# Moving the first dense layer of a gated convolution and MLP kernel into its FFT stage, handover and first period

## The chip, the cores and the metric

The kernel runs on one core of one Trainium2 chip. A core has five engines, each with an instruction queue of its own that runs in order: TensorE (matrix products, written to PSUM), VectorE and ScalarE (elementwise work), GpSimd (called POOL in the profile; here it fills buffers and issues DMA transfers) and SyncE (SP; it only issues transfers). Transfers between the chip's memory (DRAM) and the on-chip buffer are issued on the queues of SP, ScalarE and POOL. The metric is the time of one execution on the device, in microseconds; lower is better.

## The reference

A gated mix of a long convolution `a` (a diagonal state-space model, done by FFT) and a two-layer MLP `b`, and the gradients of all its inputs. L = 2048 positions, D = 448 channels, N = 256 states, F = 1792 hidden units; data in bf16.

```python
def _B_ref(x, w1, b1, w2, b2):
    h = jnp.einsum("bsd,df->bsf", x, w1) + b1
    zero = jnp.zeros_like(h)
    r = jnp.where(h > zero, h, zero)
    h = r * r
    out = jnp.einsum("bsf,fd->bsd", h, w2) + b2
    return out

x = A_u
g = _sigmoid((x * gate_w).sum(-1, keepdims=True))
a = _A_ref(x, A_A_re, A_A_im, A_B_re, A_B_im, A_C_re, A_C_im, A_log_dt, A_Dskip)
b = _B_ref(x, B_w1, B_b1, B_w2, B_b2)
return g * a + (1 - g) * b
...
_out, _vjp = jax.vjp(_f, A_u, A_A_re, A_A_im, A_B_re, A_B_im, A_C_re, A_C_im, A_log_dt, A_Dskip, B_w1, B_b1, B_w2, B_b2, gate_w)
_grads = _vjp(grad_out)
```

`_A_ref` builds the kernel K of each channel from powers of `exp(dt * A)` and convolves u with it. What matters below: `r` (the relu of the first layer, needed again in the backward pass) and `r * r`, which feeds the second product.

## The kernel before

The program has five stages. Times are those of the profiled execution.

- **Start** (to about 88 us): inputs, the gate, the first FFT step of u and of the incoming gradient (`fwd1`), and `UT`, which is u transposed, in a buffer `SB`.
- **FFT stage** (88 to 181 us; lines 560 to 626). `powers(gr)` squares a table of complex numbers twelve times, for four groups of chunks; ScalarE and VectorE take turns, and a record of each chunk goes to `rec_d`. `spectra(q)` loads a quarter of both signals from `gd`, does the second FFT step on TensorE (`fwd2`, line 265) and copies the results out of PSUM (lines 218, 219, 228, 230). `products` multiplies the two spectra on VectorE (line 288), and `inv1` does the first step back on TensorE (line 303) and stores to `hd`. In this stage the order in each queue comes from a planner, which places instructions by estimated durations. PSUM banks `X` and `S` are free here.
- **Handover** (181 to 229.6 us). From line 994 on the order is the program's own. `hd` and the record of chunk 1 are loaded on SP's queue (lines 998 and 1015), then all of w1 into `w1w` (lines 1020 to 1022). Tables for chunks 0 and 1 are built, sums of `hd` are formed on TensorE (line 1037), turned through DRAM and loaded back as `DK`.
- **Periods 1 to 13** (229.6 to 568.7 us). The 448 channels form 14 chunks. Period c builds tables of chunk c on VectorE (`X0` to `X2`, `Y0` to `Y4`: lines 656, 657, 670, 673, 679) while chunk c - 1 goes backward: `Z` is a product on TensorE and a ScalarE copy (`back_z`, lines 815 and 817), `T` turns a table (line 773), `P` multiplies on VectorE (lines 827 and 828), `S` sums on TensorE (line 844). ScalarE spreads fields and seeds for the next chunk (lines 688, 689, 709 to 724). The string `PERIOD` (line 1086) is that order written out; `KO` ends the period with a copy (`k_out`, line 760), queues the DMA transposes of the `Y` table on SP (line 779) and calls `release()`, which issues the transfers collected in `behind`. For chunks in `ON_PE` (7 to 12) one of four transposes is done on TensorE, with two ScalarE copies (line 790).
- **Tail** (to the end): weight gradients and the last FFT steps. It reads r back from `rT_d`.

At each of the ten `D` tokens of a period `D_` runs pending steps of the generator `dense()`. The first layer (`first_layer`, lines 896 to 932) runs, for each of four blocks of 512 positions (`lb`), seven steps (`jp`), each for 256 hidden units: eight matrix products (lines 905 and 908) into two PSUM banks, two relus with the bias on ScalarE (line 912), a store of r to `rT_d` on POOL's queue, and, two steps later, its square on VectorE (line 915) into `hblk`. Then `project` multiplies that block by w2 in eight half-steps (line 883), each pair ending with a ScalarE copy (line 887). During the last block's projection `turn_w1` transposes w1 (lines 940 and 941), then `turn_w2` w2. The second layer (`second_layer`) is the backward pass: 28 steps of products (lines 963 and 966), two ScalarE copies (line 968), one VectorE product with r (line 971), and the same projections with w1. In all 127 steps: eight in period 1, and the other 119 by their number, evenly over periods 2 to 13.

## Time and profile before

| | us |
|---|---|
| median of 3 runs (lowest, highest) | 812.92 (811.3, 815.8) |
| the profiled execution | 813.03 |
| its span, first to last instruction | 811.2 |

A profile line names the source line, the engine, the operation and the tiles (`out<-in`, with their types and shapes). "Idle before" is how long the engine stood just ahead of such an instruction, and the name behind the arrow is what it was waiting for. PEclk is the share of TensorE's full clock that the throttle granted: at 0.5 a matrix product takes about twice as long. PEld is TensorE's weight load, which runs beside PE. A name such as `SPq` is a queue's own time for issuing a transfer. Engines overlap, so busy times don't add up to the span; an idle engine costs only where something waits for it.

### The profile page before, as it was taken

The page shows a single profiled execution, that of the slowest core. Times are in us where ns is not written, and L with a number is a line of the kernel's source. Part 1 is how long each engine was busy: PE and PEld are TensorE (multiplying, and loading weights), DVE is VectorE, ACT ScalarE, POOL GpSimd, SP SyncE. Part 2 cuts the span into 40 slices and gives each one's busy share as a digit, 9 for nine tenths or more (in the row PEclk, how much of TensorE's full clock was granted, in tenths as well). Part 3 has the DMA queues.
Part 4 walks back from the last instruction along what each step waited for, and adds up shares of the span by engine and source line. Part 5 has one row for each costly group of instructions (what it writes and reads, how often), then busy time and mean ns, then how long its engine had stood idle before and what let it go on. Part 6 is the DMA issues. An engine that isn't in the chain of part 4 may idle for free. (4 is left out here: it accounts for less than half of the span.)

```text
span 811.2 us, 17087 instructions
## 1 busy us (share of the span) xinstructions
PE 621.9 (77%) x6845; PEld 303.0 (37%) x6845; DVE 612.7 (76%) x947; ACT 539.4 (66%) x879; POOL 162.0 (20%) x264
## 2 busy tenths in 40 slices
PE   3776367663378889988989889989778689898985
PEld 1222122121243334434554444534535234444442
DVE  3795597877834999989789989989657864888263
ACT  0696467670578687968899879884575487465463
POOL 1222000042111132213231001101135311123122
PEclk9986555565688989999989999999989899999998
DMA  9978766279759387968986979895689998999972
GB/s 192 240 204 282 298 244 233 90 286 212 211 109 186 76 198 142 200 124 217 196 158 112 290 175 228 176 246 139 207 274 311 368 294 289 285 301 330 255 218 63
DMA packets 167214, 175.73 MB, mean 217 GB/s; under 512 B 104068, under 2 KB 144990, under 8 KB 166542
## 3 DMA queue, kind: packets, MB, share of 16 engines
q1 hardware_dynamic: 140152, 97.89, 49.9%
q0 software_dynamic: 17552, 56.44, 22.8%
q10 hardware_dynamic: 9430, 20.31, 7.2%
q8 instruction: 53, 0.87, 0.5%
q14 instruction: 27, 0.22, 0.1%
HBM read 83.67 MB, written 67.53 MB: 186 GB/s over the span
## 5 line engine op out<-in xcount | busy, mean ns | idle before, releaser
L817 ACT CAST P<-psF 128x1024 bf16<-128x1024 f32 x56 | 57.2, 1021 | 27.8 <-PE psF L815 27.7
L656 DVE TENSOR_TENSOR F<-X,F 128x1024 bf16<-128x1024 bf16 (+2 forms) x42 | 64.4, 1533 | 9.8 <-ACT X L689 7.3
L883 PEld LDWEIGHTS <-U 128*128 128x128 bf16 x448 | 40.9, 100 | 48.0 <-issue 16.6
L883 PE MATMUL psN<-D,U 128*128 128x448 bf16 x224 | 54.1, 386 | 1.1 <-DMA D<-in_B_w_dram 0.7
L888 POOL DMA_DIRECT2D br_d<-D x32 | 17.5, 548 | 180.0 <-ACT D L887 173.7
L1201 PEld LDWEIGHTS <-S 128*128 128x128 bf16 x416 | 39.0, 99 | 38.6 <-issue 9.3
L1201 PE MATMUL psX<-D,S 128*128 128x449 bf16 x224 | 47.2, 353 | 1.7 <-ACT S L1207 1.5
L883 PE MATMUL psN<-S,U 128*128 128x448 bf16 x224 | 46.8, 353 | 1.5 <-issue 1.3
L963 PE MATMUL psN<-S,K 128*128 128x512 bf16 x168 | 42.4, 386 | 6.0 <-ACT R L790 5.6
L815 PE MATMUL psF<-R,S 41*32 41x256 bf16 x896 | 24.7, 291 | 28.0 <-DVE P L828 17.4
L827 DVE TENSOR_TENSOR M<-P,psF 128x2048 bf16<-128x2048 bf16 x28 | 34.1, 1216 | 14.0 <-PE psF L773 12.5
L905 PE MATMUL psN<-S,K 128*128 128x512 bf16 x168 | 43.1, 395 | 0.0
L1201 PE MATMUL psX<-K,S 128*128 128x448 bf16 x192 | 41.2, 359 | 1.7 <-ACT S L1204 1.7
L1192 ACT ACTIVATE S<-psN 128x1024 bf16<-128x1024 bf16 x32 | 33.0, 1030 | 13.7 <-PE psN L1188 13.6
L303 PE MATMUL psN<-D,cb_MI 64*128 64x448 bf16 x96 | 31.7, 532 | 9.1 <-DVE D L288 5.5
L303 PEld LDWEIGHTS <-cb_MI 64*128 64x128 bf16 x256 | 17.6, 110 | 53.2 <-issue 46.5
L265 PEld LDWEIGHTS <-M 128*64 128x64 bf16 x192 | 13.9, 133 | 62.6 <-issue 54.9
L657 DVE TENSOR_TENSOR X<-F 128x512 bf16<-128x512 bf16 (+2 forms) x42 | 35.6, 847 | 1.4
L968 ACT ACTIVATE U<-psN 128x512 bf16<-128x512 f32 x56 | 31.1, 616 | 7.6 <-PE psN L966 5.3
L796 ACT COPY S<-K 128x128 bf16<-128x128 bf16 x56 | 34.9, 1007 | 0.0
L828 DVE TENSOR_TENSOR P<-P,psF 128x2048 bf16<-128x2048 bf16 x28 | 34.2, 1221 | 1.0
L773 PE MATMUL psF<-ident,X 128*128 128x128 bf16 x448 | 31.8, 228 | 3.0 <-ACT P L817 2.9
(350 smaller groups left out, 1617.3 us busy)
## 6 DMA issues: line engine op xcount, KB each, us to landing
sp<-K ACTq DMA_DIRECT2D x8, 896.0 KB
dhT_d<-U SPq DMA_DIRECT2D x28, 256.0 KB
R<-sp SPq DMA_DIRECT2D x8, 896.0 KB
S<-dhT_d POOLq DMA_DIRECT2D x14, 512.0 KB, 7.3
R<-hd SPq DMA_DIRECT2D x16, 448.0 KB
S<-rT_d POOLq DMA_DIRECT2D x12, 512.0 KB, 7.0
hd<-st SPq DMA_DIRECT2D x13, 448.0 KB
rec<-rec_d POOLq DMA_DIRECT2D x11, 448.0 KB, 4.8
```

The costliest lines, as they stand in the source:

```text
L303: nc.tensor.matmul(ps[kk2][:, 0:D], lhsT=MI[r0:r0 + 64, m, :], rhs=rh[r0:r0 + 64], start=(k_ == 0), stop=(k_ == len(terms) - 1), tile_posi ...
L656: V.tensor_tensor(out=Vt[:, 0:2 * w * n], in0=run(lo, 0, [0, 2], [NA, w], [1, n]), in1=run(PX[:, 0:1], 512 * k, [2, w], [0, n], [1, 2]), o ...
L657: V.tensor_tensor(out=run(lo, n, [NA * X2, 2], [NA, X2], [1, n]), in0=run(vb, 0, [n * X2, 2], [n, X2], [1, n]), in1=run(vb, (w + X2) * n, ...
L796: S.copy(D2[:, :, 0, 4 * l:4 * l + 4].rearrange("p (g i) a -> p a g i", g=NG), DK[:, l::4].rearrange("p a (e g q i) -> p a e q g i", g=NG, ...
L817: S.copy(zbs[c, g // 2][:, :, g % 2].rearrange("p t h k n -> p t k h n"), psz[:].rearrange("p t (k h n) -> p t k h n", k=2, h=2))
L827: V.tensor_tensor(out=pr.rearrange("p t g h k n -> p t (g h k n)"), in0=zv, in1=xv, op=ALU.mult)
L828: V.tensor_tensor(out=zv, in0=zv, in1=rev_dim(xv, 1), op=ALU.mult)
L883: T_.matmul(ps[:, 0:D], lhsT=hblk[:, j, P * tt:P * tt + P], rhs=ws[:, j, :], start=(w == 1 and j == 0), stop=(j == FT - 1))
L905: T_.matmul(pss[k][:], lhsT=w1w[:, dt, j * P:j * P + P], rhs=UT[:, dt, 512 * lb:512 * lb + 512], start=(dt == 0), stop=False, skip_group_c ...
L963: T_.matmul(pss[k][:], lhsT=w2Tw[:, jp, dt, k], rhs=dblk[:, dt], start=(dt == 0), stop=False, skip_group_check=True)
L1192: S.activation(hn(i)[:, 8 * th:8 * th + 8, :], ps[:], ACT.Square if i < FT else ACT.Copy)
L1201: T_.matmul(ps[:, 0:w], lhsT=hn(i)[:, t, :], rhs=(DB2[:, t, :] if i < FT else U[:, t, 0:w]), start=(t == 0), stop=(t == LT - 1))
```

## The change

The 28 steps of the first layer that make r no longer run in the periods. They are now `h_step`, in the order `jp` first, then `lb`: 16 in the FFT stage (between the parts of each quarter), 4 in the handover and 8 in period 1. An `h_step` in the FFT stage does one of its two relus on ScalarE and one on VectorE; the others do both on ScalarE. Each of the seven blocks of w1 has its own buffer and its own loads of 256 columns. r goes to `rT_d`: the first eight stores of the FFT stage on POOL's queue and its other eight on SP's, those of the handover and period 1 on POOL's.

From period 2 on r is loaded back from `rT_d` on SP's queue into six buffers (and one more for the seventh tile), and ScalarE squares it into one of two blocks, during the projection of the block before. The loads that a square's buffer makes possible are collected and issued twice in a period, at `KO` and at the new token `RL`. The whole w1 load moves from the handover to the end of period 1, into the same memory. `turn_w1` runs in the first block's projection instead of the last one's. The loads `load_db` and `load_r` go on SP's queue instead of POOL's. `ON_PE` starts at chunk 2 instead of 7. The remaining steps are spread over periods 2 to 13 by weights (0.3 for the first three steps of squares, 1.0 for a half projection, 0.5 for `turn_w2`, 1.3 for a step of the second layer) instead of by number.

```diff
+    HP = FT // 2
+    W1B = ct["Ew_tile"]
+    w1bs = [RA[:, 7168:8192], SB[:, 11264:12288], Pct_[:, 7168:8192]] + [W1B[:, 4096 + 1024 * i:5120 + 1024 * i] for i in range(4)]
...
+    def load_w1b(jp, q_):
+        wb, f0 = w1bs[jp], 256 * jp
+        q_.dma_start(wb[:, 0:3], bass.AP(tensor=B_w1.tensor, offset=B_w1.offset + f0, ap=[[F, P], [P * F, 3], [1, 256]]))
+        for h in range(2):
+            q_.dma_start(wb[64 * h:64 * h + 64, 3], bass.AP(tensor=B_w1.tensor, offset=B_w1.offset + 384 * F + f0, ap=[[F, 64], [1, 256]]))
+    hleft = [(jp, lb) for jp in range(HP) for lb in range(4)]
...
+    hbanks = [lambda: K.ps("X", [P, 512]), lambda: K.ps("S", [P, 512])]
...
+    def h_step(bks, on_act, q_=None):
+
+        jp, lb = hleft.pop(0)
+        wb = w1bs[jp]
+        pss = [b() for b in bks]
+        for k in range(2):
+            for dt in range(DT - 1):
+                T_.matmul(pss[k][:], lhsT=wb[:, dt, k * P:k * P + P], rhs=UT[:, dt, 512 * lb:512 * lb + 512], start=(dt == 0), stop=False, skip_group_check=True)
+        for k in range(2):
+            h = slice(64 * k, 64 * k + 64)
+            T_.matmul(pss[k][:], lhsT=wb[h, 3, k * P:k * P + P], rhs=UT[h, 3, 512 * lb:512 * lb + 512], start=False, stop=True, tile_position=(64 * k, 0), skip_group_check=True)
+        r = hbuf[hn_[0] % len(hbuf)]
+        hn_[0] += 1
+        for k in range(2):
+            b1 = b1_f[:, 2 * jp + k:2 * jp + k + 1]
+            if on_act[k]:
+                S.activation(r[:, 512 * k:512 * k + 512], pss[k][:], ACT.Relu, bias=b1)
+            else:
+                V.tensor_scalar(out=r[:, 512 * k:512 * k + 512], in0=pss[k][:], scalar1=b1, scalar2=0.0, op0=ALU.add, op1=ALU.max)
+        (q_ or G_).dma_start(pair_rows(rT_d, jp, lb), r.rearrange("p (k l) -> p k l", k=2))
+
+    def H(n=1):
+        for _ in range(n):
+            h_step(hbanks, (True, False), nc.sync if len(hleft) <= 20 else G_)
+    for jp in (3, 4):
+        load_w1b(jp, nc.sync)
     powers(0)
     spectra(0)
     powers(1)
     for q in range(4):
         if q < 3:
             spectra(q + 1)
+        if q == 0:
+            for jp in range(3):
+                load_w1b(jp, G_)
+        H((2, 3, 3, 1)[q])
         for h in range(2):
             K.products(Pct[:, h], spw[:, 2 * (q % 2) + 1, 2 * h:2 * h + 2], spw[:, 2 * (q % 2), 2 * h:2 * h + 2])
             K.inv1(None, q, hd[0], (h,), Pct[:, h])
+            H(1 if (q, h) != (3, 1) else 0)
...
+    def load_rx(i, q):
+        if i < 4 * HP:
+            asked.append(i)
+            q.dma_start(rx_of(i).rearrange("p (k l) -> p k l", k=2), pair_rows(rT_d, i % HP, i // HP))
+
+    def square(i):
+        jp, lb = i % HP, i // HP
+        if i not in asked:
+            release()
+        assert i in asked
+        hb = hblkB if lb % 2 else hvs[0][:, 0:7168].rearrange("p (j l) -> p j l", j=FT)
+        S.activation(hb[:, 2 * jp:2 * jp + 2].rearrange("p k l -> p (k l)"), rx_of(i), ACT.Square)
+        if i != HP - 1:
+            behind.append(lambda: load_rx(i + (7 if i < HP else 6), nc.sync))
...
+        while hleft:
+            h_step([bank, bank], (True, True))
+            yield
...
+        for i in range(HP):
+            behind.append(lambda i=i: load_rx(i, nc.sync))
+        behind.append(lambda: nc.sync.dma_start(w1w[:, 0:3], bass.AP(tensor=B_w1.tensor, offset=B_w1.offset, ap=[[F, P], [P * F, 3], [1, F]])))
...
+        def ex0(k):
+            for v in (2 * k, 2 * k + 1):
+                if v < HP:
+                    turn_w1(v)
+                elif 8 <= v < 8 + HP:
+                    square(HP + v - 8)
...
+        yield from project(0, 0, w2n, ex0)
+        for lb in (1, 2):
+            yield from project(lb, 0, w2n, lambda k, lb=lb: square(HP * lb + HP + k) if k < HP else None)
+        yield from project(3, 0, w2n, ex3)
...
+    first_steps = len(hleft) - 4 + 1
+    cost = [0.3] * 3 + [1.0] * 32 + [0.5] * HP + ([1.3] * HP + [1.0] * 8) * 4
...
+    for jp in (5, 6):
+        load_w1b(jp, nc.sync)
+    del hbuf[:]
+    hbuf += [SB[:, 8192:9216], SB[:, 9216:10240], SB[:, 10752:11776]]
+    for _ in range(4):
+        h_step(hbanks, (True, True))
...
-    PERIOD = """X0 D Z0 Y0 X1 D X2 Z1 D Y1 T0 SA D P0 LR Y2 D Z2 D Y3 Z3 FX0 Y4 FX1 D S0 FY0 T1 D FY1 FY2 XS YS KM P1 YP SV D D KO S1""".split()
+    PERIOD = """X0 D Z0 Y0 X1 D X2 Z1 D Y1 T0 SA D P0 RL LR Y2 D Z2 D Y3 Z3 FX0 Y4 FX1 D S0 FY0 T1 D FY1 FY2 XS YS KM P1 YP SV D D KO S1""".split()
     nd = PERIOD.count("D")
-    ON_PE = range(7, NCH - 1)
+    ON_PE = range(2, NCH - 1)
```

More of the change, by code (lines that the diff above doesn't have):

```diff
@@ L930, in first_layer @@
             if k > 0:
-                load_r(k + 1)
+                load_r(k + 1, nc.sync)
             yield
@@ L953, in second_layer @@
     def second_layer():
-        load_r(7)
+        hblk = hvs[0][:, 0:7168].rearrange("p (j l) -> p j l", j=FT)
+        load_r(7, nc.sync)
         for lb in range(4):
@@ L984 @@
     steps = dense()
-    done, total = 0, 4 * 2 * (HP + 8) + HP
+    first_steps = len(hleft) - 4 + 1
+    cost = [0.3] * 3 + [1.0] * 32 + [0.5] * HP + ([1.3] * HP + [1.0] * 8) * 4
+    cost = [sum(cost[:i + 1]) for i in range(len(cost))]
+    done, total = 0, first_steps + len(cost)
     def D_(want):
@@ L1019 @@
     tables_y(0)
-    nc.sync.dma_start(w1w[:, 0:3], bass.AP(tensor=B_w1.tensor, offset=B_w1.offset, ap=[[F, P], [P * F, 3], [1, F]]))
-    for h in range(2):
-        nc.sync.dma_start(w1w[64 * h:64 * h + 64, 3], bass.AP(tensor=B_w1.tensor, offset=B_w1.offset + 384 * F, ap=[[F, 64], [1, F]]))
     seeds_x(1)
@@ L1070 @@
     dbl = [SB[:, 6272 + 2048 * i:8320 + 2048 * i] for i in range(2)]
-    rr = [hv[:, 7168:8192], st4] + [w2v[:, 1024 * i:1024 * i + 1024] for i in range(6)]
     xst = [0]
@@ L1149 @@
                 k += 1
-                D_(first_steps * k // nd if c == 1 else first_steps + (total - first_steps) * ((c - 2) * nd + k) // (nd * (NCH - 2)))
+                D_(first_steps * k // nd if c == 1 else first_steps + sum(x <= cost[-1] * ((c - 2) * nd + k) / (nd * (NCH - 2)) + 1e-6 for x in cost))
             elif c == 1 and o == "LR":
```

87 lines of the change are left out of this document (48 added, 39 removed).

## The prediction

> **What bounds the kernel now.** The page's first two parts come first: no engine is full over the span, and TensorE's granted clock is down between slices 4 and 12.
>
> ```profile
> PE 621.9 (77%) x6845; PEld 303.0 (37%) x6845; DVE 612.7 (76%) x947; ACT 539.4 (66%) x879; POOL 162.0 (20%) x264
> ...
> PEclk9986555565688989999989999999989899999998
> ```
>
> So the stages have different bounds. I cut the span at the FFT stage (88 to 181 us), the handover (181 to 229.6) and the ends of the 13 periods, which are the `k_out` copies of line 760 on ScalarE. In this view of windows the columns are the stretch, its length, the busy time of each engine with its count, granted clock, DMA share and GB/s.
>
> ```profile
> core 0: us, PE busy (x) PEld busy (x) DVE busy (x) ACT busy (x) POOL busy (x), PEclk, DMA share, GB/s
> 88.00:181.00 93.00, 60.21 (x240) 20.60 (x239) 75.44 (x152) 62.19 (x125) 9.23 (x8) 0.57 0.57 215
> 185.10:205.50 20.40, 8.98 (x85) 3.38 (x89) 12.94 (x15) 0.00 (x0) 2.78 (x2) 0.50 0.95 220
> 229.60:257.90 28.30, 22.08 (x312) 9.56 (x313) 8.80 (x11) 21.70 (x34) 5.42 (x7) 0.87 0.92 180
> 257.90:285.70 27.80, 24.23 (x342) 11.26 (x341) 25.50 (x30) 17.41 (x28) 4.16 (x7) 0.88 0.44 86
> 285.70:311.00 25.30, 22.60 (x309) 9.95 (x308) 24.78 (x30) 20.59 (x33) 7.06 (x11) 0.87 0.93 181
> 311.00:338.40 27.40, 25.39 (x365) 11.93 (x363) 24.83 (x29) 21.91 (x35) 6.49 (x10) 1.00 0.80 174
> 392.60:418.80 26.20, 23.38 (x405) 14.35 (x403) 22.94 (x25) 24.47 (x33) 8.03 (x13) 0.87 0.78 170
> 338.40:546.00 207.60, 183.33 (x2817) 95.12 (x2816) 191.72 (x219) 173.96 (x261) 37.73 (x64) 0.96 0.87 192
> 546.00:568.70 22.70, 21.09 (x328) 10.68 (x328) 20.64 (x23) 11.26 (x20) 3.25 (x6) 0.96 0.58 147
> 257.90:568.70 310.80, 276.64 (x4154) 138.93 (x4153) 287.46 (x328) 245.13 (x371) 58.68 (x97) 0.95 0.81 177
> ```
>
> In periods 2 to 13 (last row) VectorE is busy 287.5 of 310.8 us, 92%: it sets the pace, with TensorE (89%) close behind and ScalarE (79%) with room, but in the period that ends at 418.8 ScalarE is at 24.47 of 26.2, 93%. Period 1 has almost no VectorE work. The second row lies in the handover; two rows of SP's queue and one of ScalarE, in order of time, say what it waits for:
>
> ```profile
> 190.19 0.58 SPq L701 DMA_DIRECT2D M<-rec_d  x1
> ...
> 192.05 0.41 SPq L1020 DMA_DIRECT2D K<-in_B_w_dram  x1
> ...
> 205.53 0.83 ACT L709 COPY F<-M 128x768 bf16<-128x768 bf16 x1 [21.36 <-DMA M<-rec_d]
> ```
>
> Between 185 and 205.5 us ScalarE does nothing, until the record of chunk 1 (`rec_d`) lands behind the `hd` loads in the same queue, and the DMA engines are at 0.95: this stretch is bound by bytes, at 220 GB/s.
>
> **The change part by part.** The prices of one step are read from the groups (count, then busy time in all, mean ns of one):
>
> ```profile
> L720 ACT ACTIVATE F<-rec 128x768 bf16<-128x768 bf16 x26 | 20.7, 852 | 0.0
> L717 ACT COPY F<-rec 128x1536 bf16<-128x1536 bf16 x13 | 19.2, 1479 | 1.8 <-DVE F L673 1.8
> L912 ACT ACTIVATE S<-psN,b_f 128x512 bf16<-128x512 f32 x28 | 18.2, 712 | 3.2 <-PE psN L908 3.1
> L790 ACT COPY R<-psN 128x1024 bf16<-128x1024 bf16 x16 | 17.6, 1164 | 1.1 <-PE psN L789 1.1
> L887 ACT CAST D<-psN 128x448 bf16<-128x448 f32 x32 | 17.5, 546 | 23.1 <-PE psN L883 22.9
> ...
> L941 ACT COPY S<-psN 128x896 bf16<-128x896 bf16 x7 | 6.4, 910 | 4.5 <-PE psN L940 4.4
> ```
>
> ```profile
> L219 DVE CAST K<-psN 128x448 bf16<-128x448 f32 x22 | 13.4, 622 | 19.0 <-PE psN L265 18.8
> L971 DVE TENSOR_TENSOR U<-U,D 128x1024 bf16<-128x1024 bf16 x20 | 13.0, 684 | 1.9 <-ACT U L968 1.9
> ```
>
> One first-layer step costs 0.65 us per ScalarE relu (18.2 / 28), twice, and its square on VectorE 0.65 us (line 971 has the same form). Its TensorE price is read from two steps of period 1, one at half clock, one at full:
>
> ```profile
> 231.15 2.69 PE L905 MATMUL psN<-S,K 128*128 128x512 bf16 x6
> ...
> 234.44 1.47 PE L905 MATMUL psN<-S,K 128*128 128x512 bf16 x6
> 235.84 0.39 PE L908 MATMUL psN<-S,K 64*128 64x512 bf16 x2
> ```
>
> So 1.9 us at full clock and about 3.1 at half.
>
> *FFT stage: +5 us.* Sixteen steps come in, each with one relu on ScalarE (16 x 0.65 = 10.4 us) and one add-and-max on VectorE. The trace has no such instruction; line 219 (448 columns from PSUM, 0.62 us) scaled to 512 columns is estimated at 0.69, so 11 us. VectorE goes from 75.4 to 86.4 of 93 us, ScalarE from 62.2 to 72.6. The longest waits of VectorE there (from 89.7 us; the sum, how often, the longest):
>
> ```profile
> DVE K L219 <- PE psN L265: 11.5, 5, 9.1
> DVE R L593 <- ACT P L591: 2.7, 4, 1.0
> DVE R L593 <- ACT S L591: 2.7, 5, 1.0
> DVE D L288 <- PE psN L303: 2.5, 3, 1.4
> ```
>
> 9.1 us of it is one wait at the start for the `gd` load, the rest is pieces of 1.4 us or less. If all 11 us fill idle time the stage grows by nothing, if none do by 11; I take the middle, 5. TensorE sets a bound above: 16 x 3.1 us at the present 0.57 clock is 50 us on 60.2, 110 for 93, or +17. Against that, the period that ends at 338.4 has TensorE busy 25.39 of 27.4 us with a clock of 1.00, and at full clock the sum is 60 + 30 at most, which fits. The stores and the block loads use a DMA share of 0.57 and queues that idle.
>
> *Handover: +4.8 us.* Four steps run on TensorE and ScalarE, which idle there, so their arithmetic is free. Their four stores are not (the row of DMA issues has their size and the us to landing):
>
> ```profile
> rT_d<-S POOLq DMA_DIRECT2D x14, 256.0 KB, 5.2
> ```
>
> They leave through POOL's queue while the `hd` loads and the record saturate the DMA engines: 1.05 MB / 220 GB/s = 4.8 us. If they land outside the stretch it is 0. The whole w1 load that goes from here stood behind the record in SP's queue, so its removal gives nothing. The DMA page of the Trainium skill ("DMA: Bandwidth & Descriptors", section "Issuing engines are not separate DMA queues") says that transfers from the scalar, sync and gpsimd engines all run on the same 16 engines and interleave. By it a second queue for r adds no bandwidth, and the 0.95 share above agrees.
>
> *Period 1: 0.* Eight steps instead of seven (+1.3 us of ScalarE, which is busy 21.7 of 28.3) against half a projection less; both bounds are under 2 us.
>
> *Periods 2 to 4: +8.5 us.* Twenty-one steps go from periods 2 to 7, but all 28 squares go to ScalarE, and the new weights (0.3, 1.0, 0.5, 1.3; 104.8 in all, 8.73 a period) put 13, 8 and 7 of them in periods 2, 3 and 4, with all seven `turn_w1` in period 2. A square of 1024 columns from SBUF lies between line 720 (768 columns, 20.7 / 26 = 0.80) and line 717 (1536, 1.48): 1.0 us. `ON_PE` from 2 adds two copies of line 790, 2.2 us a period. ScalarE's own work in a period: the three rows have 59.9 us, less 14 steps' relus (28 x 0.65 = 18.2) and some 7.5 projections (x 0.55 = 4.1), over three: 12.5. Then:
> - period 2: 12.5 + 2.2 + 13 + 7 x 0.91 + 3 x 0.55 = 35.7
> - period 3: 12.5 + 2.2 + 8 + 5 x 0.55 = 25.5
> - period 4: 12.5 + 2.2 + 7 + 4 x 0.55 = 23.9
>
> That is 85.1 us of ScalarE for what took 80.5. With no gap it costs 4.6; at the 93% of the fullest period 91.5, or +11. I take 8.5, between them. A late reload holds ScalarE too: what stands behind a square on its queue is `back_z`'s copy, `back_p` on VectorE waits for that, and TensorE's next `back_z` for `back_p`. The r tiles that squares 7 to 12 free are asked for at `KO`, behind that period's transposes on SP, and square 13 is the first step of period 3:
>
> ```profile
> 278.53 16.31 SPq L779 DMA_TRANSPOSE R<-Y  x4
> ...
> 410.28 11.17 SPq L779 DMA_TRANSPOSE R<-R  x3
> ```
>
> With three transposes of 11.2 us from 7 to 9 us before a period's end, the load goes out 2 to 4 us into the next one. I put up to 5 us of this into the range.
>
> *Periods 5 to 13: -6.5 us.* VectorE's own work is (287.5 - 49 x 0.65) / 12 = 21.3 us a period. Periods 5 to 12 now hold 27 products of the second layer: 8 x 21.3 + 27 x 0.65 = 188 against 191.7 us. At the present share (191.7 / 207.6 = 92%) that is -4; with less TensorE and ScalarE work in periods 6 and 7 I take -6, up to -16.5 if VectorE runs with 1.5% gaps. Period 13 loses one product: -0.5.
>
> Sum: 5 + 4.8 + 0 + 8.5 - 6.5 = +11.8. The profiled run took 813.03 us, 1.8 more than its span of 811.2 and level with the median of the runs shown, 812.92. Forecast: **825 us**.
>
> **The rivals.**
> - *Faster, by TensorE: 805 us.* If the other engines wait for TensorE in both stages, its relief pays twice. In the FFT stage full matmuls open the clock and the waits of lines 219 and 288 on it (11.5 - 9.1 and 2.5 us) go, and with them the like on ScalarE: 0 instead of +5. In periods 5 to 12 VectorE runs nearly gapless, -16.5, and period 13 -1; periods 2 to 4 cost only ScalarE's bare content, +4.6, the handover its 4.8: -8. For it: TensorE at 89% of the periods. Against it: VectorE is at 92% already, and most of what it does stays. It decides if period 5, which has no square, falls under 22.5 us. The Trainium skill's page "TensorE: Matmul & The Clock Gate", section "What's actually happening", has the throttle released by activity; the FFT stage's 0.57 beside 0.9 to 1.0 in fuller periods agrees.
> - *No change: 815 us.* The FFT steps find their place (the 9.1 us wait among it) and the stores miss the saturated stretch, so that only the periods' +2 is left. Against it: planned places go by estimates, and the store follows its relu at once.
> - *TensorE binds the FFT stage at half clock: 837 us.* +17 instead of +5. For it: the clock is at half in most of that stage though TensorE is busy 65%, and the work comes in pieces between waits for two banks.
>
> **How the numbers follow.** Forecast 0.40, faster 0.27, no change 0.17, half clock 0.16. The range goes from 4 us under the faster case to the last one with the late reload, 801 to 842; it takes in the bounds of the FFT steps (0 to +17), of the stores (0 to 4.8), of periods 2 to 4 (+4.6 to +16) and of periods 5 to 12 (-16.5 to -4), though not all at one end. Faster or slower counts from 0.5%, 4 us, which is about what a measurement of this kernel can tell. Faster 0.27, same 0.17, slower 0.56 (forecast and half clock).
>
> **What would show it.** Right: the FFT stage 3 to 8 us longer with VectorE above 85 us; the record landing 4 to 5 us later after the last `hd` store; period 2 above 34 us with ScalarE over 90%, and periods 5 to 12 near 25. Wrong: period 2 under 31 us, where squares would cost less or lie in gaps; an FFT stage that doesn't grow; periods 5 to 12 under 24 us, where TensorE was the pace.

## The result: slower by 3.9%, and where the 36 us lie

The changed kernel takes 844.05 us (median of four runs, 837.0 to 849.34), the kernel before 812.11 beside it: ratio 1.0386, interval 1.0294 to 1.0478. The direction was forecast, the size wasn't: 825 was predicted, and 844 lies just outside the range that ended at 842.

The profiled execution took 849.34 us, with a span of 847.6 (811.2 before). Both spans are cut at the same places of the program: the FFT stage ends with the issue of its last `hd` store, and a period ends with its `k_out` copy (line 760 before, 811 after); period 1 begins at the end of the first of these copies.

| stretch | before | after | difference | forecast |
|---|---|---|---|---|
| FFT stage, to the last `hd` store | 180.8 | 203.7 | +22.9 | +5 |
| handover, to period 1 | 49.6 | 51.3 | +1.7 | +4.8 |
| period 1 | 27.9 | 28.3 | +0.4 | 0 |
| periods 2 to 4 | 80.6 | 91.6 | +11.0 | +8.5 |
| periods 5 to 13 | 230.2 | 227.6 | -2.6 | -6.5 |
| tail | 242.1 | 245.1 | +3.0 | 0 |

The tail is not touched by the change and scatters: in the eighteen runs below it took 235 to 245 us.

Of the page of the changed kernel, the busy times and the granted clock by slices:

```profile
PE 643.2 (76%) x6896; PEld 313.3 (37%) x6925; DVE 606.6 (72%) x935; ACT 566.6 (67%) x901; POOL 154.3 (18%) x254
...
PEclk9975678579858697999799989999979799999999
```

VectorE went from 76% of the span to 72% and the time still grew: some work was taken from it (612.7 to 606.6 us), and it waits longer. The view of windows, with the columns as in the prediction (the FFT stage from 89.7 us, then periods 1, 2, 3, 5 and 6, then periods 2 to 13 together):

```profile
89.70:204.00 114.30, 92.57 (x361) 28.13 (x364) 85.64 (x168) 71.10 (x138) 18.93 (x19) 0.74 0.58 211
...
254.90:283.30 28.40, 23.66 (x332) 10.04 (x337) 6.43 (x7) 22.38 (x35) 6.26 (x9) 0.82 0.84 188
283.30:324.20 40.90, 31.21 (x396) 17.05 (x396) 25.55 (x30) 34.43 (x44) 2.88 (x5) 0.79 0.89 228
324.20:351.30 27.10, 22.87 (x338) 12.49 (x339) 21.15 (x23) 24.92 (x36) 4.35 (x9) 0.87 0.63 150
...
374.80:403.50 28.70, 22.76 (x367) 12.97 (x368) 24.76 (x26) 21.23 (x31) 5.39 (x10) 0.88 0.59 152
403.50:432.90 29.40, 21.59 (x353) 11.51 (x356) 20.95 (x26) 22.85 (x35) 0.00 (x0) 0.83 0.73 137
...
283.30:602.50 319.20, 254.62 (x4037) 136.22 (x4054) 273.10 (x304) 255.28 (x365) 35.95 (x66) 0.90 0.76 179
```

**FFT stage.** VectorE gained 10.2 us (75.4 to 85.6) and ScalarE 8.9 (62.2 to 71.1), nearly what was counted. But the stage is 23 us longer, so VectorE's idle time, which was to take in part of the 10 us, grew as well: from 15.9 us (of 91.3, counted from 89.7) to 28.7.

**Period 2** takes 41 us with ScalarE busy 34.4 of them (forecast: 35.7). The content was right; the idle time around it wasn't. ScalarE's timeline at its start (start, us busy, line, in brackets how long it stood and for what):

```profile
282.79 0.48 ACT L811 CAST P<-psX 128x328 bf16<-128x328 f32 x1
285.59 3.90 ACT L973 ACTIVATE U<-S 128x1024 bf16<-128x1024 bf16 x4 [2.32 <-DMA S<-rT_d]
289.39 0.99 ACT L868 CAST P<-psF 128x1024 bf16<-128x1024 f32 x1
290.28 1.06 ACT L973 ACTIVATE U<-U 128x1024 bf16<-128x1024 bf16 x1
291.24 1.04 ACT L973 ACTIVATE U<-st 128x1024 bf16<-128x1024 bf16 x1
292.19 1.00 ACT L868 CAST P<-psF 128x1024 bf16<-128x1024 f32 x1
293.08 1.06 ACT L973 ACTIVATE U<-S 128x1024 bf16<-128x1024 bf16 x1
296.21 0.91 ACT L1030 COPY S<-psN 128x896 bf16<-128x896 bf16 x1 [2.07 <-PE psN L1029]
297.36 0.91 ACT L1030 COPY S<-psN 128x896 bf16<-128x896 bf16 x1 [0.24 <-PE psN L1029]
```

Four squares (line 973) stand ahead of the first `back_z` copy (line 868), and the first of them waits 2.3 us for its tile of r. So the copy ends at 290.4, and TensorE's next product into bank `F` waits 7.6 us for it (the longest of the eleven waits in the first row of the changed kernel's waits below).

**Periods 2 to 13** together are 8.4 us longer. Three waits there that grew (the sum, how often, the longest), first of the kernel before, then of the changed one:

```profile
PE psF L815 <- ACT P L817: 2.2, 5, 1.0
...
DVE F L656 <- ACT X L689: 7.3, 6, 2.3
...
DVE M L827 <- PE psF L773: 2.9, 3, 1.4
```

```profile
PE psF L866 <- ACT P L868: 20.8, 11, 7.6
...
DVE M L878 <- PE psF L824: 25.5, 8, 7.5
DVE F L707 <- ACT X L740: 11.5, 7, 4.8
```

These are the same three waits under new line numbers. VectorE's busy time fell by 14.4 us (287.5 to 273.1) and its idle time rose by over 22 (23.3 to 46.1): `back_p` waits for a turned table on TensorE (2.9 to 25.5 us), and TensorE waits for ScalarE to empty the bank `F` (2.2 to 20.8).

### The profile page after: what moved, and what is told of

It is laid out like the page before. It is cut to its first block, busy times and chain, and to the rows that moved or that the text cites. A ratio compares the mean times of both kernels' runs of the same rounds, so it can differ in the third digit from the quotient of the medians.

```text
span 847.6 us, 17291 instructions
## 1 busy us (share of the span) xinstructions
PE 643.2 (76%) x6896; PEld 313.3 (37%) x6925; DVE 606.6 (72%) x935; ACT 566.6 (67%) x901; POOL 154.3 (18%) x254
## 5 line engine op out<-in xcount | busy, mean ns | idle before, releaser
L868 ACT CAST P<-psF 128x1024 bf16<-128x1024 f32 x56 | 57.4, 1025 | 28.3 <-PE psF L866 26.0
L866 PE MATMUL psF<-R,S 41*32 41x256 bf16 x896 | 25.7, 302 | 48.8 <-ACT P L868 21.6
L938 PE MATMUL psN<-S,U 128*128 128x448 bf16 x224 | 50.1, 367 | 0.7 <-issue 0.3
L1053 PE MATMUL psN<-S,K 128*128 128x512 bf16 x151 | 42.8, 401 | 5.8 <-ACT R L841 3.7
L938 PEld LDWEIGHTS <-U 128*128 128x128 bf16 x336 | 30.9, 102 | 33.7 <-issue 11.3
L824 PE MATMUL psF<-ident,X 128*128 128x128 bf16 x448 | 33.8, 236 | 8.6 <-ACT P L868 8.5
L901 POOL DMA_DIRECT2D s_d<-st x21 | 11.2, 537 | 137.8 <-ACT st L899 137.8
L824 PEld LDWEIGHTS <-X 128*128 128x128 bf16 x448 | 29.8, 106 | 15.6 <-issue 15.2
L866 PEld LDWEIGHTS <-S 41*32 41x32 bf16 x896 | 9.2, 90 | 65.7 <-issue 37.5
L841 ACT COPY R<-psN 128x1024 bf16<-128x1024 bf16 x26 | 28.9, 1161 | 3.3 <-issue 2.6
## 6 DMA issues: line engine op xcount, KB each, us to landing
dhT_d<-U SPq DMA_DIRECT2D x28, 256.0 KB
D<-rT_d SPq DMA_DIRECT2D x21, 256.0 KB
```

The lines of the kernel that those rows point to most:

```text
L824: T_.transpose(ps[:, t, 128 * b:128 * b + 128], Xs[c % 2][:, o_:o_ + 128], ident[:])
L866: T_.matmul(psz[32 * ii:32 * ii + 32, t, 256 * k:256 * k + 256], lhsT=DKc[64 * t:64 * t + NY, c % 2, CW * g + i].rearrange("p s a -> p (s ...
L868: S.copy(zbs[c, g // 2][:, :, g % 2].rearrange("p t h k n -> p t k h n"), psz[:].rearrange("p t (k h n) -> p t k h n", k=2, h=2))
L938: T_.matmul(ps[:, 0:D], lhsT=hb[:, j, P * tt:P * tt + P], rhs=ws[:, j, :], start=(w == 1 and j == 0), stop=(j == FT - 1))
L1053: T_.matmul(pss[k][:], lhsT=w2Tw[:, jp, dt, k], rhs=dblk[:, dt], start=(dt == 0), stop=False, skip_group_check=True)
```

## The experiments

Each run is an edit of the changed kernel, but the one that says otherwise. The kernel before took 809.9 to 813.5 us (medians) beside them. "Last `hd` store" is the end of its issue; some of the expectations name its start (180.4 and 203.3 for the two kernels). Where an edit leaves out stores of r (e1, e2, e4, e5, e14), rows of r that nobody writes are read from written rows of the same size; this part of the edits is not printed.

| run | last hd store | period 1 begins | periods 1 to 13 | time | ratio (interval) |
|---|---|---|---|---|---|
| before | 180.8 | 230.3 | 338.8 | 812.1 | |
| after | 203.7 | 254.9 | 347.6 | 844.1 | 1.039 (1.029 to 1.048) |
| e1 no steps in the FFT stage | 186.6 | 237.3 | 347.6 | 828.9 | 1.021 (1.015 to 1.028) |
| e2 products only | 187.0 | 237.9 | 350.6 | 832.2 | 1.025 (1.017 to 1.034) |
| e3 relus only | 206.1 | 256.3 | 347.6 | 841.1 | 1.036 (1.028 to 1.044) |
| e4 no stores | 206.0 | 256.0 | 346.9 | 846.6 | 1.043 (1.038 to 1.049) |
| e5 no steps, no loads | 181.8 | 248.5 | 346.0 | 838.4 | 1.033 (1.018 to 1.049) |
| e6 relus on ScalarE | 206.1 | 254.3 | 347.0 | 846.6 | 1.044 (1.033 to 1.054) |
| e7 steps last | 189.5 | 270.8 | 346.7 | 863.7 | 1.065 (1.053 to 1.076) |
| e8 weights | 203.5 | 254.7 | 348.6 | 843.2 | 1.039 (1.028 to 1.051) |
| e9 squares on VectorE | 204.2 | 255.9 | 347.6 | 851.6 | 1.050 (1.040 to 1.060) |
| e10 ON_PE from 7 | 207.9 | 256.7 | 353.6 | 845.0 | 1.042 (1.031 to 1.053) |
| e11 eight in the handover | 206.5 | 264.4 | 350.3 | 855.9 | 1.055 (1.043 to 1.068) |
| e12 squares on GpSimd | 202.7 | 252.2 | 382.6 | 877.1 | 1.082 (1.070 to 1.093) |
| e13 one powers group | 173.3 | 221.3 | 349.1 | 815.7, one run | |
| e14 the same, no steps | 153.9 | 204.0 | 352.0 | 796.0, one run | |
| e15 r loads on POOL | 204.1 | 255.3 | 363.7 | 864.3 | 1.065 (1.060 to 1.070) |
| e16 before, half the squares on ScalarE | 182.3 | 231.4 | 335.5 | 811.1 | 0.997 (0.994 to 1.000) |
| e17 one powers group, relus only | 171.6 | 221.3 | 348.8 | 811.5, one run | |
| e18 weights and VectorE | 207.9 | 256.7 | 356.2 | 850.0 | 1.049 (1.036 to 1.062) |

The marks are of one profiled execution each and the times are of one to ten runs; a few microseconds between two rows are not to be read. The changed kernel, e8, e9, e10, e12, e15 and e18 show the size of the scatter: they are the same program up to period 1, and their last `hd` store comes at 202.7 to 207.9 us, and their handover takes 48.8 to 51.8 us.

### What of a step costs the FFT stage

Three theories: TensorE (the products and the order of its queue), the relus on VectorE and ScalarE, and the stores with their four buffers.

*e1*, the steps left out:

```diff
         jp, lb = hleft.pop(0)
+        fft = len(hleft) >= 12
+        if fft:
+            return
```

> The sixteen steps of the FFT stage are left out whole (products, relus, stores); the loads of the w1 blocks stay, and r rows that are never written are replaced by written rows of the same size. Theory 'the steps themselves': the last hd store is issued at 180 to 184 us (203.3 in the changed kernel, 180.4 before), period 1 begins near 233, the time is about 822. Rival 'the block loads and the moved buffers': the last hd store stays above 190, the time above 832.

Measured: 186.6 and 828.9, between the two. The steps make 17.1 of the 22.9 us; 5.8 stay without them. The row of its FFT stage, the control for the next two runs:

```profile
89.70:186.60 96.90, 64.32 (x248) 21.78 (x245) 75.54 (x152) 62.04 (x124) 11.68 (x11) 0.55 0.55 206
```

*e2*, the products kept, relus and stores left out:

```diff
             T_.matmul(pss[k][:], lhsT=wb[h, 3, k * P:k * P + P], rhs=UT[h, 3, 512 * lb:512 * lb + 512], ...)
+        if fft:
+            return
```

> The sixteen steps keep their products; their relus and stores are left out. Theory A, TensorE's content and its in-order queue: the last hd store stays at 195 us or later, time 836 or more. Theory B, the relus lengthen VectorE's and ScalarE's work: the last hd store at 188 or earlier, time 829 or less.

*e3*, one product for each bank instead of four, relus and stores kept:

```diff
-            for dt in range(DT - 1):
+            for dt in range(1 if fft else DT - 1):
...
-        for k in range(2):
+        for k in range(0 if fft else 2):
             h = slice(64 * k, 64 * k + 64)
```

> The sixteen steps keep relus and stores; of the eight products only one for each bank is left. Theory A (TensorE): the last hd store at 190 us or earlier, time 831 or less. Theory B (relus): it stays at 195 or later, time 836 or more.

Measured: 187.0 with the products alone, 206.1 with the relus. The windows of the FFT stage, of e2 and then of e3:

```profile
89.70:187.00 97.30, 78.83 (x376) 26.88 (x376) 75.80 (x152) 62.04 (x124) 10.84 (x11) 0.84 0.56 208
```

```profile
89.70:206.00 116.30, 79.67 (x272) 23.36 (x272) 86.95 (x168) 70.36 (x138) 18.94 (x19) 0.57 0.60 219
```

The second number is the length, then come PE, PEld, DVE, ACT and POOL, and the granted clock. The products alone raise TensorE from 64 us (e1) to 79 and the stage is no longer than without them (97.3 us against 96.9). The relus add 11.2 us to VectorE and 8.3 to ScalarE, and the stage is 19.0 us longer: about the sum of the two. So theory A falls as far as the products' own time goes, and theory B stands. One part of A comes back with the relus: in e3 TensorE stands 12.9 us for a relu to empty its bank, a wait that e2 doesn't have.

```profile
PE psS L644 <- DVE R L655: 10.3, 7, 4.4
...
PE psX L644 <- ACT R L653: 2.6, 3, 1.0
```

*e4*, the stores of the sixteen steps left out (a return ahead of the DMA in `h_step`):

> The sixteen steps keep products and relus; their stores of r are left out, so that no relu waits for a buffer. Theory C, stores and their four buffers: the last hd store 6 us or more earlier than 203.3, time 838 or less. Theories A and B: within 3 us of 203.3, because the waits of relus on stores in the changed kernel come to 4.7 us and partly lie beside others.

Measured: 206.0 and 846.6. The stores and their buffers cost nothing that shows; theory C falls.

*e5*, as e1, and five block loads less in the FFT stage:

```diff
-    for jp in (3, 4):
-        load_w1b(jp, nc.sync)
     powers(0)
...
-        if q == 0:
-            for jp in range(3):
-                load_w1b(jp, G_)
...
-    for jp in (5, 6):
+    for jp in (4, 5, 6):
         load_w1b(jp, nc.sync)
```

> As the run without the sixteen steps (last hd store issued at 186.6 us, period 1 from 237.3, time 828.9), and the loads of the five w1 blocks that belong to them are left out too (one of them goes to the handover's loads). If these loads, or the order that the planner makes around them, cost the 5 us that were left there: last hd store at 180 to 183, time 822 to 825. If it is the moved buffers: still 185 to 188, time 828 to 831.

Measured: the last `hd` store at 181.8, as before the change. So the 5 us left in e1 seem to belong to the block loads or to the order that the planner makes with them; which of the two was not separated, and 5 us is no more than the scatter of this mark. The time missed its number, for a reason that the edit made: block 4 is loaded in the handover now, the handover's steps need it, and TensorE stands for it.

```profile
PE psX L649 <- DMA U<-in_B_w_dram: 27.2, 1, 27.2
```

The handover takes 66.7 us instead of e1's 50.7: one product at the head of an in-order queue, waiting for a late load, fits these 16 us.

*e6*, both relus on ScalarE:

```diff
-            h_step(hbanks, (True, False), nc.sync if len(hleft) <= 20 else G_)
+            h_step(hbanks, (True, True), nc.sync if len(hleft) <= 20 else G_)
```

> Both relus of each of the sixteen steps on ScalarE, none on VectorE (VectorE about 12 us less, ScalarE 10 us more). Theory 'the two engines take turns, so relu time on either of them adds': last hd store at 199 to 208 us (203.3 in the changed kernel), time 839 to 850. Rival 'VectorE alone is full in the FFT stage': last hd store at 194 or earlier, time 835 or less.

Measured: 206.1 and 846.6. In its window VectorE is nearly back at what it had before (77.6 us against 75.4), and the stage is as long as ever:

```profile
89.70:206.00 116.30, 92.75 (x374) 28.82 (x373) 77.59 (x152) 80.15 (x154) 18.94 (x19) 0.78 0.59 215
```

So VectorE's content isn't the limit: the same relus cost the same on either engine, within the scatter of the mark. Against e2, ScalarE has 18.1 us more and VectorE 1.8, and the stage is again 19.0 us longer: once more about what was added to the two engines together.

*e7*, the sixteen steps behind the FFT stage in the program (`H(16)` after the loop over the quarters, the calls in it taken out). The planner still put some of the work into gaps; 14 of the 16 ScalarE relus and 11 of the 16 VectorE relus run after the stage's end:

> The sixteen steps stand behind the whole FFT stage in the program, so that the planner puts four into a gap and twelve behind the last products. Theory 'steps stand ahead of the stage's own chain': last hd store of the stage 184 to 192 us, the twelve run while the handover waits for the loads of hd and the record, period 1 begins at 240 to 248 (254.9), time 829 to 838. Rival 'the steps need their time wherever they stand': period 1 begins at 253 or later, time 842 or more.

Measured: the stage ends at 189.5, as expected, but period 1 begins at 270.8, 16 us later than in the changed kernel. What TensorE and ScalarE wait for between 189.5 and the end of the `hd` sums at 249.6, and the row of this stretch:

```profile
PE psX L643 <- ACT S L652: 8.8, 3, 7.3
PE psX L643 <- ACT R L652: 3.8, 4, 2.0
```

```profile
ACT R L652 <- PE psX L646: 19.7, 10, 4.7
ACT F L652 <- PE psX L646: 7.3, 4, 2.3
```

```profile
189.50:249.60 60.10, 46.98 (x245) 14.70 (x245) 25.40 (x32) 22.59 (x34) 13.31 (x14) 0.80 0.65 190
```

The first of these waits is no mark of the move: it belongs to the handover's own four steps, and the changed kernel has the same 8.8 us there. Where the steps run (189.5 to 228.1 us) TensorE is busy 34.3 of 38.6 us and the relus wait for its products, 27.0 us on ScalarE alone. Here a step costs its products: 2.1 us from one ScalarE relu to the next once the granted clock is 1.00 (from 210 us on), 2.3 to 5.4 before 205 us, where it is at 0.50 to 0.53. In a row the steps are longer than the wait that they were to hide in, and they hold up its loads too: the record of chunk 1 is asked for on SP's queue at 227.2 us instead of 212.9, behind eight stores of r that wait for their relus. Which of the two sets the 16 us was not tried.

*e11* moves four steps only, into the handover's own row:

```diff
-        H((2, 3, 3, 1)[q])
+        H((1, 2, 2, 0)[q])
...
-    for _ in range(4):
+    for _ in range(8):
         h_step(hbanks, (True, True))
```

> Twelve steps in the FFT stage instead of sixteen, eight in the handover instead of four. A step in the FFT stage costs some 1.15 us by the runs so far (18 us for sixteen), so the last hd store comes at 198 to 201 us (203.3). If the handover hides four more behind its wait for the record: period 1 begins at 249 to 252 (254.9), time 838 to 841. If it doesn't (they need TensorE and two banks, about 2.6 us each in the run with the steps last): period 1 at 256 to 262, time 845 or more.

Measured: 206.5 and 264.4. The handover is 6.7 us longer, 1.7 us for each of the four steps. Here the round trip through the two banks does show: a step's products take TensorE 1.8 us, then it waits 0.8 us for the relu that empties the bank, and the last five ScalarE relus of bank `X` follow each other by 2.6 to 3.9 us. The FFT stage with twelve steps is no shorter than with sixteen, against the expected 198 to 201; the 3 to 5 us that were looked for are of the size of the scatter, so this neither shows nor refutes a constant price of 1.15 us a step.

### Is it the chain of powers?

ScalarE and VectorE take turns in `powers`, which would make time on either of them add. *e13* leaves out three of its four groups, *e14* the steps as well, *e17* keeps the steps' relus but one product for each bank:

```diff
-    powers(1)
...
-        if q < 2:
-            powers(q + 2)
...
-        ... offset=c * P * RS, ap=[[RS, P], [1, RS]]))
+        ... offset=c % 4 * P * RS, ap=[[RS, P], [1, RS]]))
```

> The changed kernel without three of the four groups of powers (records of chunks 4 to 13 are read from the first group's rows), the sixteen steps kept. To be read against the run without these groups and without the steps. Theory 'the powers' alternation between VectorE and ScalarE makes relu time add': without most of that chain the steps lie in idle time, the last hd store of the two runs differs by 8 us or less (17 with the powers: 203.7 against 186.6). Rival 'something else of the stage (products, banks, queue order) makes them add': still 14 us or more.

> The same without three groups of powers, and without the sixteen steps (their rows of r replaced by written rows): the control. The stage falls below 186.6 us at its last hd store if the powers are its chain (theory: 165 or less); if it stays above 178, the powers were not what bounded it.

> One group of powers, the sixteen steps with relus and stores but one product for each bank instead of four; between the control without steps (last hd store 153.9) and the run with full steps (173.3). Theory 'relus add only where the powers make VectorE and ScalarE wait for each other; without powers it is TensorE's content': 160 or less. Rival 'relus add in full in any case': 168 or more.

Measured: 173.3, 153.9 and 171.6. The windows of e13, e14 and e17:

```profile
89.70:173.30 83.60, 76.06 (x367) 25.10 (x371) 61.39 (x91) 38.83 (x68) 21.23 (x21) 0.87 0.70 247
```

```profile
89.70:153.90 64.20, 49.99 (x247) 18.82 (x248) 48.23 (x75) 30.67 (x55) 14.10 (x13) 0.74 0.69 253
```

```profile
89.70:171.60 81.90, 69.49 (x277) 20.44 (x277) 59.89 (x91) 38.41 (x68) 20.20 (x21) 0.68 0.70 252
```

The powers do bound the stage (186.6 falls to 153.9 without three groups, far below the 165 of the expectation). But the steps still add 19.4 us, and the relus with two products 17.7, with ScalarE busy less than half the time. So the theory falls: it is not the powers' alternation that makes relus dear. What is shown is that the relus with their waits cost this stage 17 to 19 us, on either engine and with four groups of powers or one.

The rows allow one more reading. Each time relus come in, the stage grows by nearly all the busy time that they add to VectorE and ScalarE together, as if nothing of it overlapped: 19.0 us for 19.5 (e2 to e3), 19.0 for 19.9 (e2 to e6), 17.7 for 19.4 (e14 to e17), 17.1 for 19.2 (e1 to the changed kernel). A step costs some 1.1 us and has two relus, so a relu costs 0.5 to 0.6 us, which is no more than its own busy time (0.69 us on ScalarE, 0.75 on VectorE); no wait has to be added to explain it. Why nothing overlaps, on engines that idle a quarter and over a third of the stage, stays open. The two engines' exchange of work beyond the powers, TensorE standing for its banks, and the order that the planner makes around the relus all fit, and no run holds that order fixed.

### The periods

*e8*, levelled weights:

```diff
-    cost = [0.3] * 3 + [1.0] * 32 + [0.5] * HP + ([1.3] * HP + [1.0] * 8) * 4
+    cost = [1.6] * 3 + [2.4, 1.8, 1.8, 1.3] + [2.0] * 3 + [1.4] + ([1.6] * HP + [1.0]) * 2 + [1.0] * 8 + [0.9] * HP + ([1.6] * HP + [1.0] * 8) * 4
```

> Only the weights of the steps in periods 2 to 13 are changed, so that period 2 holds 7 squares and the seven turns of w1 instead of 13 squares and these. Theory 'ScalarE's content binds period 2': period 2 at 33 to 37 us (41.0), periods 2 to 6 together 138 to 146 (149.6), time 834 to 841. Rival 'the loads of r and w1 are late': period 2 stays at 39 or more.

Measured: period 2 at 33.2 us, periods 2 to 6 at 141.5, both as expected; and 843.2 us in all, as before the edit. Its windows of periods 2 to 4:

```profile
283.00:316.20 33.20, 22.61 (x336) 13.99 (x336) 25.23 (x30) 27.07 (x35) 1.80 (x3) 0.69 0.88 242
316.20:343.00 26.80, 22.05 (x350) 11.56 (x348) 21.07 (x23) 25.20 (x35) 3.78 (x7) 0.87 0.54 114
343.00:371.40 28.40, 19.94 (x324) 10.90 (x324) 22.01 (x24) 23.31 (x32) 2.71 (x5) 0.88 0.75 180
```

ScalarE lost 7.4 us in period 2 and the period 7.8. But TensorE lost 8.6 as well (31.2 to 22.6), because steps of products moved with the squares, so this doesn't show which of the two set the length. And what left came back later: periods 7 to 13 took 178.8 us instead of 169.6, and the time missed its 834 to 841.

*e9*, the squares on VectorE (`V.tensor_tensor` with `rx_of(i)` twice instead of `S.activation`), and *e18*, this with the weights of e8:

> All 28 squares of periods 2 to 5 on VectorE instead of ScalarE (some 28 us less ScalarE, 18 us more VectorE). Theory S, 'what stands on ScalarE's queue ahead of the copies that the chain needs sets periods 2 to 4': periods 2 to 4 together 80 to 87 us (91.6 in the changed kernel), time 834 to 841. Rival 'VectorE sets the pace, as in the kernel before': periods 2 to 4 at 91 or more, time 844 or more.

> The levelled weights and the squares on VectorE together. Theory 'the work of a period adds up over the engines that exchange it, whichever does it': periods 1 to 13 at 344 to 350 us (347.6), time 840 to 847. Rival 'ScalarE's load in period 2 and the late turn of w1 were what kept them': 340 or less, time 836 or less.

Measured: periods 2 to 4 at 91.7 us and periods 1 to 13 at 347.6 in e9, the same numbers as in the changed kernel, and 851.6 us in all, as the rival had it; 356.2 in e18, worse than either theory had it. Theory S falls as a cause of the sum: 25 us off ScalarE and 16 onto VectorE (255.3 to 230.3 and 273.1 to 288.7 in periods 2 to 13) move single periods (period 2 fell to 36.7, 3 to 5 grew by 6.2 together) and leave the total. Period 2 of e9:

```profile
282.20:318.90 36.70, 27.80 (x369) 15.21 (x369) 29.79 (x37) 22.31 (x31) 2.90 (x5) 0.76 0.90 226
```

ScalarE has 12.1 us less there than in the changed kernel (34.4) and the period is only 4.2 shorter, with no engine busy for more than 82% of it. So ScalarE's content alone didn't set it either.

*e10*, `ON_PE = range(7, NCH - 1)`:

> Only the set of chunks with a transpose on TensorE is put back (7 to 12 instead of 2 to 12): in periods 2 to 6 ScalarE loses two copies of about 1.1 us each, TensorE sixteen transposes, and SP issues a fourth DMA transpose. Theory S: periods 2 to 6 together 140 to 146 us (149.6), time 835 to 842. Rival 'the transposes land late and delay the next period's first product': periods 2 to 6 at 149 or more.

Measured: periods 2 to 6 at 151.1 us. Two copies less a period on ScalarE, with the fourth DMA transpose back on SP's queue, buy nothing.

*e15*, the loads of r on POOL's queue (`G_` instead of `nc.sync` in `load_rx`, `load_r` and `load_db`):

> The loads of r and of the transposed second signal for the dense layers go on POOL's queue instead of SP's, as in the kernel before. Theory 'loads behind the transposes are late and the transposes behind the loads too': periods 2 to 6 together 143 us or less (149.6), period 6 near 26 (29.3), time 838 or less. Rival 'the chain of copies and products sets them': periods 2 to 6 at 147 to 153, time 841 or more.

Measured: slower, 864.3, period 2 at 50.0 us and periods 2 to 6 at 158.0, beyond both theories. ScalarE's timeline at the start of period 2:

```profile
284.32 0.43 ACT L811 CAST P<-psX 128x328 bf16<-128x328 f32 x1
293.22 1.06 ACT L973 ACTIVATE U<-S 128x1024 bf16<-128x1024 bf16 x1 [8.46 <-DMA S<-rT_d]
295.24 1.06 ACT L973 ACTIVATE U<-S 128x1024 bf16<-128x1024 bf16 x1 [0.96 <-DMA S<-rT_d]
297.11 2.08 ACT L973 ACTIVATE U<-S 128x1024 bf16<-128x1024 bf16 x2 [0.82 <-DMA S<-rT_d]
299.10 0.99 ACT L868 CAST P<-psF 128x1024 bf16<-128x1024 f32 x1
```

The first square waits 8.5 us instead of 2.3, and the `back_z` copy behind it starts at 299.1, 14.3 us after period 2 began, instead of 6.1. On POOL's queue the loads of r stand behind the store of the last relu and go out at 285.4 us, 0.7 us into the period; on SP's queue they went out from 280.9, 2.4 us before it. They also arrive later: the first square starts 7.8 us after the first issue instead of 4.7. This is the dependence that the forecast put up to 5 us on: a late tile of r stops ScalarE's whole queue. On SP's queue the wait is 2.3 us.

*e12*, the squares on GpSimd (`G_.tensor_tensor`):

> All 28 squares on GpSimd, which is busy 3 to 6 us of a period. Theory S: with 28 us less on ScalarE and nothing more on VectorE, periods 2 to 4 together 76 to 84 us (91.6), time 828 to 838, if a square takes under 2.5 us there. Rival: VectorE's own products get longer while GpSimd computes, or the squares and the transfers behind them on its queue come late: periods 2 to 4 at 88 or more.

Measured: 877.1, periods 2 to 4 at 119.5 us. Most squares take 1.9 to 2.4 us there, which the expectation allowed for. The rival came true. Groups of VectorE's instructions in the periods that hold the squares (busy, mean ns), of e12 and then of the changed kernel:

```profile
L851 DVE TENSOR_TENSOR S<-S,vw 128x512 bf16<-128x512 bf16 x4 | 14.3, 3578 | 0.0
L707 DVE TENSOR_TENSOR F<-X,F 128x4096 bf16<-128x4096 bf16 x4 | 13.9, 3470 | 0.1
L879 DVE TENSOR_TENSOR P<-P,psF 128x2048 bf16<-128x2048 bf16 x8 | 9.8, 1221 | 0.3
...
L708 DVE TENSOR_TENSOR X<-F 128x2048 bf16<-128x2048 bf16 x4 | 8.0, 2012 | 0.1
...
L707 DVE TENSOR_TENSOR F<-X,F 128x2048 bf16<-128x2048 bf16 x5 | 6.1, 1226 | 0.2
```

```profile
L707 DVE TENSOR_TENSOR F<-X,F 128x4096 bf16<-128x4096 bf16 x5 | 11.5, 2293 | 0.2
L879 DVE TENSOR_TENSOR P<-P,psF 128x2048 bf16<-128x2048 bf16 x8 | 9.8, 1221 | 0.3
...
L707 DVE TENSOR_TENSOR F<-X,F 128x2048 bf16<-128x2048 bf16 x5 | 6.1, 1226 | 0.2
...
L708 DVE TENSOR_TENSOR X<-F 128x2048 bf16<-128x2048 bf16 x4 | 4.9, 1225 | 0.1
```

*e16*, the kernel before, with 12 of its 28 squares on ScalarE:

```diff
-                    V.tensor_tensor(out=hblk[:, 2 * jp:2 * jp + 2]..., in0=r, in1=r, op=ALU.mult)
+                    hb = hblk[:, 2 * jp:2 * jp + 2].rearrange("p k l -> p (k l)")
+                    if jp % 2:
+                        S.activation(hb, r, ACT.Square)
+                    else:
+                        V.tensor_tensor(out=hb, in0=r, in1=r, op=ALU.mult)
```

> The kernel before, with 12 of its 28 squares on ScalarE instead of VectorE (VectorE 8 us less, ScalarE 12 us more in periods 1 to 7). Theory 'VectorE paces these periods (92% busy), ScalarE has room': periods 1 to 7 together 183 to 187 us (188.9), time 806 to 810. Rival 'work in front of the exchange on either engine costs': periods 1 to 7 at 188 or more, time 811 or more.

Measured: 811.07 us, ratio 0.997 with an interval that touches 1 (ten runs). Periods 1 to 7 of the kernel before, and of e16, in the view of windows:

```profile
229.60:418.80 189.20, 166.73 (x2423) 81.43 (x2424) 155.80 (x178) 147.96 (x218) 44.91 (x70) 0.91 0.80 163
```

```profile
231.40:417.70 186.30, 161.12 (x2392) 80.36 (x2406) 148.79 (x167) 157.37 (x230) 44.93 (x70) 0.94 0.79 168
```

VectorE lost 7.0 us and, from copy end to copy end, the seven periods 2.5 (188.9 to 186.4) in this execution, which the times can't tell from nothing. So VectorE, though 92% busy, is at most in part the pace. No version here that does all the work is faster than the kernel before by more than the measurement can tell; e16 is the nearest.

## Why the prediction failed, step by step

- **FFT stage, +5 against +22.9: the term that failed.** Its step was "If all 11 us fill idle time the stage grows by nothing, if none do by 11; I take the middle". The contents were right (VectorE 85.6 against 86.4, ScalarE 71.1 against 72.6). The bound of 11 us was wrong, because it counted VectorE's relus alone. The ScalarE relus (10.4 us) were put at nothing, since ScalarE had room; but e6 shows that a relu costs as much there as on VectorE, and e3 against e2 shows the stage longer by 19.0 us where the two engines were given 11.2 and 8.3. With both in it the bound would have been 21, and the steps took 17.1 of it. Why neither engine's idle time took any of it in stays open. And "the block loads use ... queues that idle" missed the 5 us that seem to come with these loads (e1 against e5).
- **TensorE at half clock (a rival, +17).** Its size was close and its mechanism wrong: the products alone cost nothing (e2), and they raised the granted clock from 0.55 (e1) to 0.84.
- **Handover, +4.8 against +1.7.** The copy of the record of chunk 1 starts 26.4 us after the last `hd` store instead of 24.7 (205.53 - 180.8). That is the sign that was forecast, but not shown: the same handover took 48.8 to 51.8 us in seven executions, against 49.6 before. No run shows a cost of 4.8 us for the stores.
- **Period 1, 0 against +0.4.** Right.
- **Periods 2 to 4, +8.5 against +11.0.** The size is within its bounds (+4.6 to +16). ScalarE's content was sized well (35.7, 25.5 and 23.9 us against 34.4, 24.9 and 22.9); its share in period 2 was not 93% but 84, with waits for r and for the turns of w1 among the rest. That ScalarE's content sets these periods, as the sum had it, is not shown: e8 took work off TensorE too, and without its squares (e9) the three periods took 91.7 us all the same. So the number came out near for a reason that the runs don't bear out, which is luck in part.
- **Periods 5 to 13, -6.5 against -2.6.** VectorE's content of periods 5 to 12 was sized at 188 us and came to 186.3; that periods shrink with it failed in periods 5 and 6 (28.7 and 29.3, 54.2 together before), and held in 7 to 13 (169.6 against 176.0). The step "at the present share" took VectorE for the pace. The waits say otherwise: it gave up 14.4 us of work over periods 2 to 13 and idled 22 longer.
- **Signs named beforehand.** VectorE above 85 us in the FFT stage, period 2 above 34 us and periods 5 to 12 near 25 (mean 25.6) came true; a stage only 3 to 8 us longer, the record 4 to 5 us later and ScalarE over 90% in period 2 did not.

Open: why the relus' time on VectorE and on ScalarE adds in full to this stage, and why periods 1 to 13 take 346 to 354 us in every run of the changed kernel but e12, e15 and e18, 7 us and more above the kernel before, whether ScalarE or VectorE squares and however the steps are spread.

## What to carry to other kernels

Idle time of an engine is not by itself room for more work. Where engines hand work to each other in in-order queues, put the busy time of an inserted step on all of them into the upper bound, not only that on the fullest one: here the stage grew by 17 to 19 us for 19 to 20 us of relus put on two engines that both had idle time. Where steps follow each other through the same banks, price them by their round trip: 2.6 us a step in e11's handover, of which 1.8 are products. When work is taken off the busiest engine, look for the wait that will take its place before counting the gain; here VectorE lost 14 us of work and gained 22 of waiting. And a tile that is stored early to be read back must be there before the first instruction of a queue that others hang on: the same square waited 2.3 us on one load queue and 8.5 on another.

## What was not expected of the hardware

- **More products, faster clock, no cost.** Sixteen steps of eight products on an FFT stage in which TensorE had a granted clock of 0.55 (e1) took the clock to 0.84 and the stage not a microsecond further (e2: 97.3 us; 96.9 without them). With two products a step instead of eight (e3) it is at 0.57. The page "TensorE: Matmul & The Clock Gate" of the Trainium skill, section "What's actually happening", says that activity releases the throttle; the three windows agree.
- **GpSimd beside VectorE.** In the periods in which GpSimd squares, several of VectorE's products with both operands in the on-chip buffer took longer on average (2293 to 3470 ns at line 707, 1225 to 2012 at line 708; at line 851 0.42 us became 3.58), and those with one operand in PSUM did not (line 879, 1221 ns in both). The Trainium skill's page "SBUF — State Buffer", section "SBUF: two separate sides", describes a port pair that GpSimd and a two-input VectorE operation can only have one at a time; the rows agree, and e12's timeline does in detail. The longest product of line 851 (8.07 us, from 317.98) ends 0.3 us after four squares in a row (318.31 to 325.76). Lines 878 and 879, with an operand in PSUM, run from 392.19 to 394.67 wholly beside two squares (392.09 to 395.84) and take their usual 1.22 us each. Line 707's products of 128x2048 kept their 1226 ns because they were first: three of them start 0.4 to 0.6 us ahead of a square (281.00 against 281.55, 337.61 against 338.03, 368.22 against 368.84).
